# Casting the two weight matrices to bf16 inside their loads, on the GpSimd DMA queue, in a fused recurrence and feed-forward kernel

## The chip, the cores and the metric

The kernel runs on one core of a Trainium2 chip. The metric is the device time of one execution in microseconds (us). The kernel before took 201.83 us, the median of three runs (200.89 to 202.03).

Engine names in the profile: PE is TensorE, PEld its weight loads, DVE VectorE, ACT ScalarE, POOL GpSimd, SP SyncE. "L189" is line 189 of that kernel's source; the line numbers differ from kernel to kernel. All times inside a profile count from the start of the profiled span. For a program on one core, a run more than 1.5% above the fastest run of the same kernel is called slow.

## The reference

```python
# q, k, v, alpha: (4 batches, 8 heads, 768 steps, 48), float32
state = zeros((B, H, 48, 48))
for t in range(768):
    state = alpha[:, :, t, :, None] * state + einsum('bhd,bhe->bhde', k[:, :, t], v[:, :, t])
    y[:, :, t] = einsum('bhd,bhde->bhe', q[:, :, t], state)
x = y.transpose(0, 2, 1, 3).reshape(3072, 384)
h = x @ w_in                 # w_in: 384 x 2048, float32
r = maximum(h, 0)
out = (r * r) @ w_out        # w_out: 2048 x 384; out: 3072 x 384, float32
```

## The kernel before

The recurrence is computed in 24 chunks of 128 steps (6 for each batch). Chunk s gives 128 rows of x, which are kept transposed in `xT_big`. Each chunk needs four loads of 192 KB (alpha, q, k and v, called `at`, `qt`, `kt`, `vt`), in rows of 48 floats, which are 192 bytes. The first matmul (x by w_in) starts with a group of four chunks, so it needs chunks 0 to 3 and the first quarter of w_in.

A list scheduler in Python, `Plan`, holds every operation with an estimated duration and its dependencies, and decides the order on each engine. The DMA loads are issued in a fixed order:

```python
    def add_loads(s):                       # four loads of chunk s, on the SP queue
        ...
        for nm, src in srcs:                # at, qt, kt, vt
            def ld(nm=nm, src=src):
                d[nm] = loads.tile([P, H, D], FP32, name=nm)
                nc.sync.dma_start(out=d[nm], in_=src[b, c])
    ...
    DMA_ORDER = [0, 1, 2, 3, "i", "i", "i", 4, "i", "o", "o", 5, "o", "o"]
    for d in DMA_ORDER + [s for s in range(NT) if s not in DMA_ORDER]:
        if d == "i":
            load_w_in(len(w_in_ready))      # a quarter of w_in, 768 KB
        elif d == "o":
            load_w_out(len(w_out_ready))    # a quarter of w_out, 768 KB
        else:
            add_loads(d)
            add_chunk(d)
```

The weights come through float32 staging tiles and are cast to bf16 by VectorE or GpSimd, whichever the scheduler finds free:

```python
    def cast(dst, box, j, d, n):
        def e_cast():
            eng = nc.vector if op.eng == "DVE" else nc.gpsimd
            pin(eng.tensor_copy(dst, box["t"][:, j, :]))
        op = add({"DVE": 0.06 + n / 1840.0, "POOL": 0.05 + n / 660.0}, 0, e_cast, d, prio=1.0)
        return op

    def load_w_in(i):
        ...
        def ld():
            box["t"] = wload.tile([P, KT * d_ff // NWP], FP32, name="wst").rearrange(...)
            nc.sync.dma_start(out=box["t"], in_=w_in_r[:, :, sl])
        d = add("DMA", WLD, ld, lat=2.0)
        cs = []
        for j in range(KT):
            cs.append(cast(w_in_b[:, j, sl], box, j, d, 512))
        w_in_ready.append(cs)
    # load_w_out: the same with w_out and four casts of 128 x 384
```

## Time and profile before

| stage of the profiled span (199.3 us) | what happens | what limits it |
|---|---|---|
| 0 to 20 us | loads of chunks 0 to 3, and their recurrence | the chunk loads: 4.2 us for each chunk |
| 20 to 26.5 us | chain of chunk 3, first casts | chunk 3's chain, with casts inside it |
| 26.5 to 44 us | first group of the first matmul | TensorE, with some waits for VectorE |
| 44 us to the end | both matmuls, remaining chunks | TensorE |

The first view is the timeline of GpSimd in the kernel before. Its columns are start, duration, engine, source line, operation, written tile <- read tile with shapes, the count, and in brackets how long the engine sat idle just before and what ended that.

```profile
7.02 0.61 POOL L284 CAST vb<-vt 128x384 bf16<-128x384 f32 x1 [3.64 <-DMA vt<-in_v_dram]
11.23 0.79 POOL L284 CAST vb<-vt 128x384 bf16<-128x384 f32 x1 [3.60 <-DMA vt<-in_v_dram]
15.45 0.61 POOL L284 CAST vb<-vt 128x384 bf16<-128x384 f32 x1 [3.43 <-DMA vt<-in_v_dram]
19.87 0.51 POOL L284 CAST vb<-vt 128x384 bf16<-128x384 f32 x1 [3.81 <-DMA vt<-in_v_dram]
```

`vt` is the last load of each chunk, so these four casts show when chunks 0 to 3 were complete: every 4.2 us, 1.05 us for one load. GpSimd waits for data each time; the loads are the limit here.

The next view is the timeline of VectorE in the kernel before, in the two places where casts of weights stand in the way.

```profile
22.65 0.43 DVE L221 CAST w_in_b<-wst 128x512 bf16<-128x512 f32 x1 [0.88 <-DMA wst<-in_moe_w_in_dram]
22.99 1.28 DVE L353 TENSOR_TENSOR sm<-sc,utri_b 128x512 bf16<-128x512 f32 x2
25.03 1.18 DVE L221 CAST w_in_b<-wst 128x512 bf16<-128x512 f32 x2 [0.76 <-DMA wst<-in_moe_w_in_dram]
26.13 0.34 DVE L408 COPY xT_big<-bank 128x384 bf16<-128x384 bf16 x1
...
41.06 2.27 DVE L221 CAST w_out_b<-wst 128x384 bf16<-128x384 f32 x5
43.25 0.35 DVE L408 COPY xT_big<-bank 128x384 bf16<-128x384 bf16 x1
```

VectorE waits 0.88 us for a weight transfer in order to cast it, while chunk 3's `sm` work stands behind the cast. Two more casts hold `xT_big` of chunk 3 until 26.13, and five casts of w_out hold another `xT_big` until 43.25. What TensorE pays for it is in its timeline in the kernel before:

```profile
26.53 0.81 PE L189 MATMUL bank<-xT_big,w_in_b 128*128 128x512 bf16 x3 [0.58 <-DVE xT_big L408]
...
28.87 0.32 PE L189 MATMUL bank<-L_s,utri_b 128*128 128x384 bf16 x1 [0.24 <-ACT L_s L278]
...
41.46 0.32 PE L189 MATMUL bank<-w_out_b,gT 128*128 128x384 bf16 x1 [0.56 <-DVE w_out_b L221]
43.66 0.34 PE L189 MATMUL bank<-L_s,utri_b 128*128 128x384 bf16 x1 [1.87 <-DVE xT_big L408]
```

The first line is the start of the first matmul, at 26.53 (its view is cut at 27 us, so the count stops at 3). The second is the first work of chunk 4. From there to the end of the span are 172.8 us. TensorE is close to full in the long stage after that, as the table of stretches shows (stretch, length, busy time of PE, PEld, DVE, ACT and POOL with their counts, granted clock, DMA share, GB/s):

```profile
60.00:176.00 116.00, 115.39 (x1349) 88.96 (x1348) 85.13 (x161) 89.87 (x272) 75.05 (x122) 1.00 0.71 137
```

Two lines of the page of the kernel before complete the picture: the span, and the clock granted to TensorE in 40 slices of 5 us, in tenths. The 7 is the slice after the wait of 1.87 us.

```profile
span 199.3 us, 5199 instructions
...
PEclk9999999997999999999999999999999999999999
```

### The profile page before, as it was taken

How to read it: one execution, taken by the hardware profiler on the slowest of the kernel's cores; microseconds unless marked ns; L12 is line 12 of the kernel's file. 1: busy time of each engine (PE TensorE's matmuls, PEld its weight loads, DVE VectorE, ACT ScalarE, POOL GpSimd, SP SyncE). 2: the span in 40 equal slices, each digit the busy share in tenths (PEclk: the TensorE clock that was granted, in tenths of full speed). 3: DMA queues.
4: the chain of work that ended last, by engine and by line, in shares of the span. 5: the costliest groups of instructions: out<-in, count | busy, mean ns of one | idle time of the engine just before them, and what ended most of it. 6: DMA issues, size and time to landing. Idle time of an engine off the chain costs nothing.

```text
span 199.3 us, 5199 instructions
## 1 busy us (share of the span) xinstructions
PE 186.2 (93%) x1926; PEld 131.4 (66%) x1926; DVE 131.0 (66%) x253; ACT 129.1 (65%) x376; POOL 105.8 (53%) x175
## 2 busy tenths in 40 slices
PE   7887779959999999999999999999999999999993
PEld 2454434437667778778777777777777777777761
DVE  0598659987839969878786576677666766723300
ACT  3466148737158669977869778877877776656510
POOL 5111366844509518678557747756766565455300
PEclk9999999997999999999999999999999999999999
DMA  6999999999859999999998999971001101100122
GB/s 128 189 187 168 349 246 318 251 272 235 157 133 219 170 194 202 202 200 199 189 211 157 226 204 202 200 163 43 22 17 44 39 3 41 44 20 20 44 79 79
DMA packets 107034, 30.23 MB, mean 152 GB/s; under 512 B 100352, under 2 KB 105472, under 8 KB 107008
## 3 DMA queue, kind: packets, MB, share of 16 engines
q1 hardware_dynamic: 107008, 29.89, 73.2%
q8 instruction: 15, 0.25, 0.6%
q14 instruction: 11, 0.09, 0.2%
HBM read 25.17 MB, written 4.72 MB: 150 GB/s over the span
## 4 chain that ended last, share of the span: by engine, by line
PE 76%; SPq 9%; DVE 6%; DMA 5%; ACT 2%; issue 1%; ACTq 0%
PE bank L189 65%; SPq L264 8%; PE bank L192 6%; DMA at<-in_alpha_dram 5%; PE sc L189 3%; DVE w_out_b L221 2%; DVE gT L453 1%; PE st L189 1%; SPq L232 1%; ACT r L446 1%; DVE qkT L337 1%; DVE sm L353 1%; DVE w_in_b L221 1%; ACT A L301 0%; DVE kI_s L323 0%
## 5 line engine op out<-in xcount | busy, mean ns | idle before, releaser
L453 POOL TENSOR_TENSOR gT<-r 128x256 bf16<-128x256 bf16 (+2 forms) x128 | 83.9, 665 | 57.9 <-ACT r L446 55.8
L446 ACT ACTIVATE r<-bank 128x256 bf16<-128x256 f32 (+2 forms) x192 | 68.9, 387 | 28.2 <-PE bank L189 25.6
L189 PE MATMUL bank<-xT_big,w_in_b 128*128 128x256 bf16 (+2 forms) x576 | 81.7, 275 | 1.1 <-DVE xT_big L408 0.6
L189 PE MATMUL bank<-w_out_b,gT 128*128 128x384 bf16 x384 | 75.2, 328 | 0.6 <-DVE w_out_b L221 0.6
L189 PEld LDWEIGHTS <-w_in_b 128*128 128x128 bf16 x576 | 49.2, 99 | 14.9 <-issue 2.4
L189 PEld LDWEIGHTS <-gT 128*128 128x128 bf16 x384 | 36.6, 98 | 17.2 <-issue 0.3
L453 DVE TENSOR_TENSOR gT<-r 128x256 bf16<-128x256 bf16 (+2 forms) x64 | 29.1, 464 | 17.6 <-ACT r L446 15.5
L353 DVE TENSOR_TENSOR sm<-sc,utri_b 128x512 bf16<-128x512 f32 x48 | 31.0, 684 | 4.4 <-PE sc L189 3.9
L320 DVE TENSOR_TENSOR qA_s<-qt,A 128x384 bf16<-128x384 f32 x24 | 13.6, 568 | 16.6 <-ACT A L301 16.6
L284 POOL CAST vb<-vt 128x384 bf16<-128x384 f32 x24 | 13.7, 573 | 18.8 <-DMA vt<-in_v_dram 18.7
L337 DVE COPY qkT<-bank 128x1024 bf16<-128x1024 bf16 x24 | 16.4, 684 | 4.7 <-PE bank L192 4.3
L484 ACT COPY ob<-bank 128x384 f32<-128x384 f32 x19 | 9.1, 481 | 13.9 <-PE bank L189 12.9
L323 DVE TENSOR_TENSOR kI_s<-kt,Ainv 128x384 bf16<-128x384 f32 x24 | 16.8, 699 | 1.9 <-ACT Ainv L305 0.4
L189 PEld LDWEIGHTS <-qkT 64*128 64x128 bf16 (+1 forms) x272 | 11.0, 95 | 9.3 <-DVE qkT L337 3.7
L301 ACT ACTIVATE A<-bank 128x384 bf16<-128x384 f32 x24 | 11.8, 493 | 7.2 <-PE bank L189 7.2
L278 ACT ACTIVATE L_s<-at 128x384 bf16<-128x384 f32 x24 | 12.5, 522 | 5.0 <-DMA at<-in_alpha_dram 5.0
L397 ACT CAST xn<-bank 128x384 bf16<-128x384 f32 x24 | 11.5, 479 | 4.8 <-PE bank L189 4.7
L379 ACT CAST sb<-st 128x384 bf16<-128x384 f32 x20 | 9.6, 478 | 7.1 <-DVE st L374 7.0
L189 PE MATMUL bank<-warm 128*128 128x512 bf16 x38 | 11.9, 453 | 1.3 <-DVE ae_s L182 1.3
L408 DVE COPY xT_big<-bank 128x384 bf16<-128x384 bf16 x24 | 8.5, 352 | 5.7 <-PE bank L192 5.6
L305 ACT ACTIVATE Ainv<-bank 128x384 bf16<-128x384 f32 x24 | 11.9, 494 | 0.0
L189 PE MATMUL sc<-qkT 64*128 64x128 bf16 x192 | 9.5, 219 | 1.9 <-DVE qkT L337 1.8
(40 smaller groups left out, 150.1 us busy)
## 6 DMA issues: line engine op xcount, KB each, us to landing
at<-in_alpha_dram SPq DMA_DIRECT2D x24, 192.0 KB, 4.6
qt<-in_q_dram SPq DMA_DIRECT2D x24, 192.0 KB, 4.5
kt<-in_k_dram SPq DMA_DIRECT2D x24, 192.0 KB, 4.6
vt<-in_v_dram SPq DMA_DIRECT2D x24, 192.0 KB, 4.3
out_dram<-ob SPq DMA_DIRECT2D x24, 192.0 KB, 2.5
wst<-in_moe_w_in_dram SPq DMA_DIRECT2D x4, 768.0 KB, 6.5
wst<-in_moe_w_out_dram SPq DMA_DIRECT2D x4, 768.0 KB, 7.9
```

The costliest lines, as they stand in the source:

```text
L189: pin(nc.tensor.matmul(*a, **kw))
L192: pin(nc.tensor.transpose(*a))
L264: nc.sync.dma_start(out=d[nm], in_=src[b, c])
L278: pin(nc.scalar.activation(L[:, :, 0:D], d["at"], AF.Ln))
L284: pin(nc.gpsimd.tensor_copy(d["vb"], d["vt"]))
L305: pin(nc.scalar.activation(d["Ai"], d["pm"][:, 0:HD].rearrange("p (h d) -> p h d", h=H), AF.Exp, scale=-1.0))
L320: pin(nc.vector.tensor_mul(qA[:, :, 0:D], d["qt"], d["A"]))
L323: pin(nc.vector.tensor_mul(kI[:, :, 0:D], d["kt"], d["Ai"]))
L337: pin(nc.vector.tensor_copy(d["qkT"], d["pT"]))
L353: pin(nc.vector.tensor_mul(d["sm"][:, hh], d["sc"][:, hh], utri_b.to_broadcast([P, NP, P])))
L446: pin(nc.scalar.activation(box["r"][:, 0:n], box["ph"][:, 0:n], AF.Relu))
L453: pin(eng.tensor_mul(gT[g][:, f, 0:n], box["r"][:, 0:n], box["r"][:, 0:n]))
```

## The change

The idea is to drop work from VectorE and GpSimd. A DMA issued from GpSimd can convert its data, so w_in and w_out are loaded straight into the bf16 tiles. The 28 casts and the four staging tiles go away; 18 of the casts ran on VectorE and 10 on GpSimd. The Trainium skill ("DMA: Bandwidth & Descriptors", SWDGE vs HWDGE vs iDMA) lists the cast in a transfer as possible from GpSimd only, so the eight weight loads have to leave the SP queue.

```diff
-    wload = ctx.enter_context(tc.tile_pool(name="wload", bufs=4))
...
-    def cast(dst, box, j, d, n): ...
+    W_EARLY = 1.5
+    W_ISSUE = 1.0
+
+    def load_w(dst, src, ready):
+        def ld():
+            nc.gpsimd.dma_start(out=dst, in_=src)
+        d = add("DMA", WLD, ld, lat=2.2)
+        d.late = -W_EARLY
+        d.pool = W_ISSUE
+        ready.append([d])
 
     def load_w_in(i):
         w = d_ff // NWP
         sl = slice(i * w, (i + 1) * w)
-        box = {}
-        (staging tile, nc.sync.dma_start, three casts)
+        load_w(w_in_b[:, :, sl], w_in_r[:, :, sl], w_in_ready)
 
     def load_w_out(i):
         w = FT // NWP
-        (staging tile, nc.sync.dma_start, four casts)
+        sl = slice(i * w, (i + 1) * w)
+        load_w(w_out_b[:, sl, :], w_out_r[:, sl, :], w_out_ready)
```

(The lines in parentheses stand for code that is cut here. A few lines in the scheduler reserve 1 us of GpSimd for each issue.)

The plan still believes in one DMA queue in the order of `DMA_ORDER`, but the load instruction is not pinned to its place. In the compiled program GpSimd's order is: the v cast of chunk 0, w_in 0 and 1, the v cast of chunk 1, w_in 2 and 3, w_out 0 and 1, the v cast of chunk 2, w_out 2 and 3, then the rest. No load waits for anything except its place in this order.

## The prediction

> **What bounds it now.** Three stages (timeline, windows).
> - 0 to 20 us: the loads of chunks 0 to 3. The GpSimd timeline shows the four vb casts waiting for v at 7.0, 11.2, 15.45 and 19.9: 4.2 us per chunk, about 1.05 us per 192 KB load, at 188 GB/s. All run in 192 B pieces; the DMA row reads 9, so I take the transfer engines to be full.
> - 20 to 44 us: chunk 3's chain, then the first group of the first matmul, starting at 26.5 (wait on xT_big). Here the casts cost time. VectorE waits 0.88 us for a w_in transfer and casts it while chunk 3's sm work is ready, so sm starts at 23.0 instead of 21.8; two more casts hold xT_big to 26.1. I estimate 2 us lost before 26.5. From 32 to 40 VectorE is 8.00 of 8 us busy, and TensorE waits 0.56 and 1.87 us near 41 to 43.7. TensorE idle from 26.5 to 44: about 3.3 us.
> - 44 to 196: TensorE is full (115.4 of 116 us in 60 to 176) and is the chain. Nothing saved elsewhere counts there.
>
> **What changes.** 28 casts go: 18 on VectorE (about 10 us), 10 on GpSimd (about 7 us). At most about 5 us lies on the chain. The eight 768 KB weight loads leave the SP queue for the GpSimd queue; the source bytes stay. In the compiled order two w_in loads follow the first vb cast, w_in 2,3 and w_out 0,1 the second, w_out 2,3 the third, all without waits. So they issue from 7.6 us on, ahead of most of chunks 1 to 3; before, the first was issued at 17.0, behind all sixteen.
>
> The Trainium skill ("DMA: Bandwidth & Descriptors", Issuing engines are not separate DMA queues) says that all queues interleave on the same 16 engines. So the second queue brings no bandwidth; it takes away the order. One weight piece costs 2.2 us of all engines (w_in pieces landed at 22.65, 25.0, 27.2), so eight cost 17.8 us. Chunk 3 landed at 19.9; if the two queues share evenly in time it lands near 30; if 2 KB pieces alternate with 192 B pieces, near 37; if the small loads win, near 20. The matmul start follows about 4.5 us later: 34, 41 or 24.5. After that about 3.3 us of gaps are won back.
>
> Sum: even sharing 201.8 + 7.5 - 3.3 = 206; alternating pieces 213; small loads winning 197 to 198; a casting transfer that is itself slower, more.
>
> **Predicted: 207 us, 197 to 217 in 8 of 10. Faster by over 2%: 0.13; within 2%: 0.30; slower by over 2%: 0.57.**
>
> **What would show it.** vb casts waiting for v well after 11.2, 15.45 and 19.9 (chunk 3 at 28 to 37); first w_in matmul at 32 to 42, ending its wait on xT_big, not on weights; the DMA row above 200 GB/s from 9 us on. From there to the end about 167 us instead of 170: no 1.87 us gap, VectorE not full.
>
> **What would make it wrong.** The small loads may be limited by their descriptors' generation rather than by the engines; then weights fill free slots, the matmul starts near 24.5 to 26, and the result is 2 to 3% faster. Or the casting transfer is much slower than 2.2 us, and the matmul or the second matmul waits for w_in or w_out: slower than 213. Or TensorE, left idle, restarts at a lower clock (0.7 in the slice after the 1.87 us gap).

## More of the kernel before

Where a chunk's chain leaves TensorE idle in the plan, the kernel issues filler matmuls on a tile of zeros, called `warm`; they keep TensorE busy and compute nothing:

```python
            if pe_end is not None and DUMMY:
                n = max(0, int((op.start - pe_end - 0.5) / 0.22))
                ...
                for _ in range(n):
                    mm(wp, lhsT=warm[:, 0:P], rhs=warm, start=True, stop=True)
```

Two pools matter later: `loads` has 6 buffers for each of the four chunk tiles, and `opool` has 4 buffers of `ob`, the output tile of one block of 128 rows. The stores of `ob` are issued on the same SP queue as the chunk loads.

## The result, and the profile after

The changed kernel took 208.68 us, the median of four runs (208.39 to 208.82), and the kernel before 201.38 us over its four runs (200.89 to 202.03). The ratio is 1.035, with a 95% interval of 1.032 to 1.038: slower. Ratios here are formed from the fast runs alone, so they are not quite the ratios of the medians quoted.

GpSimd's timeline after the change, which answers to the four lines of before. The lines "DMA_DIRECT2D" are the issues of the weight loads.

```profile
7.11 0.50 POOL L270 CAST vb<-vt 128x384 bf16<-128x384 f32 x1 [3.73 <-DMA vt<-in_v_dram]
7.55 1.71 POOL L224 DMA_DIRECT2D w_in_b<-in_moe_w_in_dram  x2
11.15 0.50 POOL L270 CAST vb<-vt 128x384 bf16<-128x384 f32 x1 [1.89 <-DMA vt<-in_v_dram]
11.60 1.55 POOL L224 DMA_DIRECT2D w_in_b<-in_moe_w_in_dram  x2
13.15 1.52 POOL L224 DMA_DIRECT2D w_out_b<-in_moe_w_out_dram  x2
28.36 0.51 POOL L270 CAST vb<-vt 128x384 bf16<-128x384 f32 x1 [13.69 <-DMA vt<-in_v_dram]
28.81 1.48 POOL L224 DMA_DIRECT2D w_out_b<-in_moe_w_out_dram  x2
32.11 0.51 POOL L270 CAST vb<-vt 128x384 bf16<-128x384 f32 x1 [1.82 <-DMA vt<-in_v_dram]
```

Chunk 1 is complete as before, at 11.15. Six weight loads are then under way, and chunk 2 comes at 28.36 instead of 15.45, chunk 3 at 32.11 instead of 19.87. VectorE, which before was held up by casts, now waits for chunk 2 (its timeline after):

```profile
21.01 0.56 DVE L306 TENSOR_TENSOR qA_s<-qt,A 128x384 bf16<-128x384 f32 x1 [7.03 <-DMA qt<-in_q_dram]
26.47 0.56 DVE L309 TENSOR_TENSOR kI_s<-kt,Ainv 128x384 bf16<-128x384 f32 x1 [4.91 <-DMA kt<-in_k_dram]
...
37.69 0.36 DVE L394 COPY xT_big<-bank 128x384 bf16<-128x384 bf16 x1 [1.28 <-PE bank L193]
```

One load of 192 KB now lands 5.46 us after the one in front of it (q at 21.01, k at 26.47), where that took 1.05 us before. TensorE's timeline after shows the same waits and the start of the first matmul:

```profile
15.11 0.48 PE L190 MATMUL bank<-L_s,utri_b 128*128 128x384 bf16 x1 [2.60 <-ACT L_s L264]
...
21.62 0.61 PE L193 MATMUL bank<-ident_bf,qA_s 128*128 128x128 bf16 x4 [3.58 <-DVE qA_s L306]
...
27.09 0.61 PE L193 MATMUL bank<-ident_bf,kI_s 128*128 128x128 bf16 x4 [4.86 <-DVE kI_s L309]
...
38.10 2.10 PE L190 MATMUL bank<-xT_big,w_in_b 128*128 128x512 bf16 x9
```

The first matmul starts at 38.10, and it waits for no weight. The chain of work that ended last goes through the same place: two of its pieces in order of time (start, duration, what) follow; the first is chunk 2's v, 15.68 us from issue to landing:

```profile
12.63 15.68 DMA vt<-in_v_dram
28.31 0.05 issue
```

The span and the clock row of the page after the change:

```profile
span 207.0 us, 5206 instructions
...
PEclk9997556999999999999999999999999999999998
```

Three stretches of the table of stretches after the change, with the columns as before:

```profile
15.00:20.00 5.00, 2.93 (x21) 1.52 (x20) 0.00 (x0) 2.00 (x7) 0.00 (x0) 0.70 1.23 198
...
25.00:30.00 5.00, 2.00 (x20) 1.50 (x21) 2.02 (x5) 0.53 (x1) 1.64 (x3) 0.50 1.10 193
...
60.00:176.00 116.00, 115.30 (x1335) 87.57 (x1334) 82.36 (x157) 88.93 (x267) 67.62 (x111) 1.00 0.65 127
```

The granted clock is at one half from 21.4 to 35.0 us and in one earlier window (14.6 to 18.0), which fits the waits of 2.6 to 4.9 us above. The long stage is unchanged: 115.30 us of 116 busy, against 115.39.

The balance of the two profiled spans is therefore short. The first matmul starts 11.6 us later (38.10 against 26.53). From there to the end the new kernel takes 168.9 us against 172.8, so 3.9 us are won back: the wait of 1.87 us and its dip of the clock are gone, and VectorE is no longer full from 32 to 40 us. The sum is 7.7 us, the difference of the spans.

The trace also has a record for every DMA packet. A packet of a chunk load is one row of 192 bytes and took 18.2 ns on average. A packet of a staged w_in load was 2048 bytes and took 100.0 ns. In the converting load, the same 512 floats arrive as a record of 1024 written bytes and took 98.2 ns, and a w_out row (768 bytes written) 80.6 ns. These means are near each other because some staged packets took much longer than most; the medians are 84 ns staged and 96 ns converting. In four slices of 2 us, from 17.6 to 25.6 us, I counted 309, 320, 383 and 381 weight packets against 323, 333, 381 and 389 chunk packets. In that stretch the two queues were served packet for packet. Earlier they were not: in the slices from 11, 13 and 15 us, 234, 281 and 262 weight packets passed beside 563, 584 and 707 chunk packets, and the trace does not tell whether every engine had both kinds waiting there.

### The profile page after: what moved, and what is told of

The parts are those of the page before. It is cut to its first block, busy times and chain, and to the rows that moved or that the text cites. A ratio compares the mean times of both kernels' runs of the same rounds, so it can differ in the third digit from the quotient of the medians.

```text
span 207.0 us, 5206 instructions
## 1 busy us (share of the span) xinstructions
PE 186.5 (90%) x1924; PEld 132.0 (64%) x1924; DVE 121.6 (59%) x239; ACT 130.3 (63%) x380; POOL 98.5 (48%) x165
## 2 busy tenths in 40 slices
DMA packets 107034, 27.08 MB, mean 131 GB/s; under 512 B 100352, under 2 KB 107008, under 8 KB 107008
## 4 chain that ended last, share of the span: by engine, by line
PE 76%; DMA 8%; SPq 5%; ACT 5%; DVE 3%; issue 1%; POOL 0%; ACTq 0%; DVEq 0%
PE bank L190 65%; DMA vt<-in_v_dram 8%; PE bank L193 6%; SPq L250 5%; PE sc L190 3%; ACT r L432 2%; PE st L190 1%; DVE kI_s L309 1%; DVE qA_s L306 1%; ACT L_s L264 1%; ACT ob L470 1%; DVE st L360 1%; ACT sb L365 0%; ACT xn L383 0%; DVE qkT L323 0%
## 5 line engine op out<-in xcount | busy, mean ns | idle before, releaser
L439 POOL TENSOR_TENSOR gT<-r 128x256 bf16<-128x256 bf16 (+2 forms) x120 | 78.5, 664 | 67.4 <-ACT r L432 62.8
L190 PE MATMUL bank<-xT_big,w_in_b 128*128 128x256 bf16 (+2 forms) x576 | 80.3, 272 | 0.5 <-ACT r L432 0.4
L190 PEld LDWEIGHTS <-w_in_b 128*128 128x128 bf16 x576 | 48.3, 97 | 14.0 <-issue 1.3
L306 DVE TENSOR_TENSOR qA_s<-qt,A 128x384 bf16<-128x384 f32 x24 | 14.4, 599 | 25.5 <-ACT A L287 18.4
L270 POOL CAST vb<-vt 128x384 bf16<-128x384 f32 x24 | 12.4, 515 | 29.3 <-DMA vt<-in_v_dram 29.3
L470 ACT COPY ob<-bank 128x384 f32<-128x384 f32 x23 | 11.1, 484 | 13.1 <-PE bank L190 12.2
L383 ACT CAST xn<-bank 128x384 bf16<-128x384 f32 x24 | 11.6, 482 | 6.4 <-PE bank L190 6.4
L193 PE MATMUL bank<-ident_bf,kI_s 128*128 128x128 bf16 x96 | 9.8, 227 | 5.9 <-DVE kI_s L309 5.9
L193 PE MATMUL bank<-ident_bf,qA_s 128*128 128x128 bf16 x96 | 9.7, 227 | 3.8 <-DVE qA_s L306 3.8
```

The lines of the kernel that those rows point to most:

```text
L190: pin(nc.tensor.matmul(*a, **kw))
L193: pin(nc.tensor.transpose(*a))
L270: pin(nc.gpsimd.tensor_copy(d["vb"], d["vt"]))
L306: pin(nc.vector.tensor_mul(qA[:, :, 0:D], d["qt"], d["A"]))
L439: pin(eng.tensor_mul(gT[g][:, f, 0:n], box["r"][:, 0:n], box["r"][:, 0:n]))
L470: pin(nc.scalar.copy(box["ob"], box["po"]))
```

## The experiments

The main theory, "order": on a second queue the weight loads overtake chunks 2 to 4, and because packets of the two queues are taken in equal numbers, each small packet of a chunk waits for a large one of the weights. The first rival, "conversion": the converting transfer is slow in itself. The second rival, "generation": the small packets come slowly by themselves, whatever else is moving. The clock is a possible third contributor.

Several experiments read float32 weights in place: w_in and w_out are loaded unchanged, and the matmul reads the upper 16 bits of each float as bf16. This drops the lower 16 bits; every run below still gave a result that passed the comparison with the reference. The kernel before ran beside the experiments on the same chip: its median was 200.89 us beside e1 to e4, 200.67 beside e5 to e8, and 201.30 beside e9 to e11. The diffs of e1 to e9 are against the changed kernel, those of e10 and e11 against the kernel before; `d.pos` fixes the place of a load in the emitted order.

| run | what it is | median us | ratio to before (95%) | first matmul at, us |
|---|---|---|---|---|
| after | the change | 208.68 | 1.035 (1.032 to 1.038) | 38.10 |
| e1_casts_gone | no casts, order as before | 199.46 | 0.994 (0.988 to 0.999) | 26.02 |
| e2_plain_pool | GpSimd queue, no conversion | 210.87 | 1.049 (1.043 to 1.054) | 38.80 |
| e3_sp_early | one queue, weights early | 211.76 | 1.056 (1.049 to 1.062) | 37.31 |
| e4_late | the change, loads behind chunk 3 | 200.80 | 0.998 (0.993 to 1.004) | 28.09 |
| e5_after_warm | the change, TensorE kept busy | 207.52 | 1.034 (1.027 to 1.041) | 36.92 |
| e6_small_rows | the change, half-width w_in rows | 212.05 | 1.056 (1.048 to 1.064) | 42.44 |
| e7_ordered | loads in order, fillers | 201.65 | 1.005 (0.998 to 1.013) | 26.82 |
| e8_hybrid | w_in in place on SP, w_out converting | 200.59 | 0.997 (0.990 to 1.004) | 25.95 |
| e9_ordered_ob8 | e7 with 8 output tiles | 198.27 | 0.986 (0.982 to 0.991) | 27.45 |
| e10_inplace | before, w_in in place, fillers | 197.77 | 0.984 (0.979 to 0.988) | 25.94 |
| e11_inplace_nofill | the same without fillers | 197.65 | 0.985 (0.979 to 0.990) | 25.02 |

(The row of after was measured earlier, against 201.38 us of before. Medians are over all runs; e2 and e8 have one slow run each, and their fast runs alone have medians of 210.77 and 200.31 us. The starts of the first matmul are each from one profiled run.)

### e1: only the casts taken away

```diff
-    w_in_b = consts.tile([P, KT, d_ff], BF16)
-    w_out_b = consts.tile([P, FT, d_model], BF16)
+    w_in_f = consts.tile([P, KT, d_ff], FP32)
+    w_out_f = consts.tile([P, FT, d_model], FP32)
+    def halves(t):
+        return t.bitcast(BF16).rearrange("p k (f two) -> p k f two", two=2)[:, :, :, 1]
+    w_in_b = halves(w_in_f[:, :, :])
+    w_out_b = halves(w_out_f[:, :, :])
...
-            nc.gpsimd.dma_start(out=dst, in_=src)
+            nc.sync.dma_start(out=dst, in_=src)      # dst is the float32 tile
```

> The casts alone are taken away: the weights stay fp32 in SBUF, loaded by the same queue in the same order as before the change, and TensorE reads the upper two bytes of each element in place (a truncation instead of a rounding, so the result is less exact). My theory (the casts cost about 5 us on the chain, the order of the loads costs about 12): first w_in matmul at 24.5 to 25.5 us instead of 26.5, no 1.87 us gap near 42, total 196 to 198 us. Rival (the casts were off the chain and the gain inside the changed kernel has another source, such as the new order of instructions): 200 to 202 us. Check: w_in and w_out matmuls must keep their 0.216 us and 0.16 us pace, else the reading in place costs something itself.

It took 199.46 us, 0.6% under the kernel before (the interval, 0.988 to 0.999, just leaves out 1), and I expected 196 to 198; the first matmul came at 26.02, and I expected 24.5 to 25.5. Chunks came as before (v casts up to 20.23). Two things took the rest. TensorE waited 1.11 us for chunk 3's k and had one window of 3.41 us at half clock. And reading w_out in place is not free. These are the two matmul groups of this run (count, then busy us, mean ns of one, then idle before):

```profile
L195 PE MATMUL bank<-xT_big,w_in_f 128*128 128x256 bf16 (+2 forms) x576 | 80.5, 272 | 0.7 <-ACT r L435 0.6
L195 PE MATMUL bank<-w_out_f,gT 128*128 128x384 bf16 x384 | 77.4, 330 | 0.0
```

In the changed kernel, which reads packed bf16, the same groups are:

```profile
L190 PE MATMUL bank<-xT_big,w_in_b 128*128 128x256 bf16 (+2 forms) x576 | 80.3, 272 | 0.5 <-ACT r L432 0.4
L190 PE MATMUL bank<-w_out_b,gT 128*128 128x384 bf16 x384 | 74.8, 326 | 0.0
```

w_in is the stationary operand (`lhsT`) and its matmuls are unchanged. w_out is the moving operand, and its group is 2.6 us longer. From the first matmul (26.02) to the end of the span (197.3) this run takes 171.3 us against 172.8 before; without the 2.6 us it would be 168.7, an estimate that agrees with the 168.9 us of the change. This fits the reading that what the change won after its first matmul is what the casts had cost.

### e2: the second queue without the conversion

The loads stand at the same places of GpSimd's order as in the change, but they carry plain float32, read in place as in e1.

```diff
-            nc.gpsimd.dma_start(out=dst, in_=src)
+            pin(nc.gpsimd.dma_start(out=dst, in_=src))   # dst float32
+        d.pos = W_POS[...]   # W_POS = [7.6, 7.7, 11.9, 12.0, 12.1, 12.2, 16.1, 16.2]
```

> The changed kernel with the conversion taken out of the transfer: the same eight weight loads at the same places of the GpSimd queue, but plain fp32 into fp32 tiles read in place. My theory (the loads overtake chunks 2 to 4, the conversion is free): as the changed kernel, vb casts of chunks 2 and 3 at 28 and 32 us, first w_in matmul at 37 to 39, total 207 to 210 us. Rival (the converting transfer is what is slow): weight packets get clearly shorter, chunk 2 lands before 24 us, total under 204 us.

It took 210.87 us, a little over the 207 to 210 expected; the first matmul, at 38.80, came as expected. GpSimd's timeline gives chunks 2 and 3 within 0.4 us of the change:

```profile
28.74 0.51 POOL L277 CAST vb<-vt 128x384 bf16<-128x384 f32 x1 [14.07 <-DMA vt<-in_v_dram]
...
32.25 0.63 POOL L277 CAST vb<-vt 128x384 bf16<-128x384 f32 x1 [1.57 <-DMA vt<-in_v_dram]
```

The rival "conversion" falls: without any conversion the loss is the same, and the 2.2 us by which this run is longer than the change are about the price of reading w_out in place (2.6 us in e1; the two totals come from different calls). The records here are of 4096 and 4608 bytes, 189 and 219 ns each, and 171, 161 and 149 of them passed in three slices of 2 us beside 185, 175 and 164 chunk packets. So in this stretch it is the number of packets that is shared equally, not bytes and not time.

### e3: the early order on one queue

```diff
-    DMA_ORDER = [0, 1, 2, 3, "i", "i", "i", 4, "i", "o", "o", 5, "o", "o"]
+    DMA_ORDER = [0, 1, "i", "i", "i", "i", "o", "o", 2, 3, "o", "o", 4, 5]
```

Everything is on the SP queue, plain float32, read in place. The weights simply go first: in the trace no chunk packet was served between 12 and 22 us.

> No GpSimd queue and no conversion: plain loads on the SP queue, six weight loads put into its order before chunk 2 and two behind chunk 3 (read in place, as in e1). My theory (order alone): six pieces of 2.2 us stand before chunk 2, so the vb cast of chunk 2 comes at about 28.7 us, of chunk 3 at about 32.9, first w_in matmul at 37 to 38, total 207 to 210 us. Rival (the loss comes from the second queue, its software descriptors or GpSimd's time): with one queue it is gone, total 197 to 202 us.

It took 211.76 us, over the 207 to 210 expected (w_out is read in place here too, and TensorE waited 1.36 us more at 39.48, for alpha of chunk 4). The first matmul, at 37.31, came as expected, and chunks 2 and 3 came where one queue in this order puts them:

```profile
28.85 0.51 POOL L273 CAST vb<-vt 128x384 bf16<-128x384 f32 x1 [17.07 <-DMA vt<-in_v_dram]
32.67 0.51 POOL L273 CAST vb<-vt 128x384 bf16<-128x384 f32 x1 [3.31 <-DMA vt<-in_v_dram]
```

The change behaves like this kernel. That follows from its order: by the time chunk 2 is complete, six weight loads are complete too, whether they ran before the chunk's packets or between them. Six loads at 2.2 us are 13.2 us, and 15.45 + 13.2 gives 28.7 against 28.36 measured. "Generation" is answered by the change itself together with this run: chunk 3, with the engines to itself, takes 3.8 us here for four loads, and in the change a single load beside the weights takes 5.46 us. Small loads limited by their own generation would have kept their pace.

### e4: the change with its loads behind chunk 3

```diff
-            nc.gpsimd.dma_start(out=dst, in_=src)
+            pin(nc.gpsimd.dma_start(out=dst, in_=src))
+        d.pos = W_POS[...]   # all eight between 20.45 and 20.8, behind chunk 3's v cast
```

> The changed kernel with all eight casting loads held in GpSimd's order behind the vb cast of chunk 3. My theory (packets of the two queues alternate one for one): chunk 3's vb cast is back at 19.9 to 20.5 us, first w_in matmul at 25 to 26.5; but then chunk 4 on the SP queue shares packet for packet with the weights and lands only at 40 to 46 us, and TensorE, which has chunk 4's transposes in its fixed order, stalls some 5 to 8 us around 32 to 42; total 200 to 205 us. Rival A (only the loads before chunk 3 matter): total 195 to 198 us. Rival B (casting loads are slow wherever they stand): 207 us or more.

It took 200.80 us, the same as the kernel before within the interval. The loss is gone with the order alone: chunk 3 came at 20.71 (GpSimd's timeline). But now the first matmul waits for its weights, 2.91 us, and starts at 28.09 (TensorE's timeline), not at 25 to 26.5 as I expected; the clock is at one half from 28.3 to 31.7 us.

```profile
20.71 0.51 POOL L272 CAST vb<-vt 128x384 bf16<-128x384 f32 x1 [4.61 <-DMA vt<-in_v_dram]
...
28.09 3.80 PE L190 MATMUL bank<-xT_big,w_in_b 128*128 128x512 bf16 x9 [2.91 <-DMA w_in_b<-in_moe_w_in_dram]
```

My expectation that chunk 4 would come late, at 40 to 46 us, was wrong: most of its packets had passed before the first weight packet. The run also showed a later wait of 2.1 us for an output copy, which e7 explains.

### e5: the clock

```diff
+    def fill(n):
+        t = banks[4].tile([P, 512], FP32, name="bank4")
+        for _ in range(n):
+            mm(t, lhsT=warm[:, 0:P], rhs=warm, start=True, stop=True)
...     # for chunk 2 alone: fill(10), fill(15) and fill(20) in its three waits
```

> The changed kernel with 45 filler matmuls on data that is already there, put where TensorE waited for chunk 2's loads (10 before the prefix product, 15 before the transposes of q, 20 before those of k), so that it does not idle. They must not delay anything: the waits there were 2.6, 3.6 and 4.9 us. If the halved clock of 20 to 34 us lengthened chunk 3's chain, the granted clock stays at 1.0, the vb casts stay at 28.4 and 32.1 us, and the first w_in matmul moves from 38.1 to 36.6 to 37.0 us; total 1.0 to 1.5 us below the changed kernel's 208.7, so 207.0 to 207.7. Rival (the clock costs nothing there because the chain waits on other engines): start unchanged within 0.3 us.

It took 207.52 us. The clock stayed at full speed, as the table of stretches of this run shows (third column from the end):

```profile
20.00:25.00 5.00, 3.40 (x20) 1.51 (x18) 0.56 (x1) 0.00 (x0) 0.00 (x0) 1.00 1.26 185
25.00:30.00 5.00, 3.30 (x29) 1.73 (x28) 2.16 (x5) 0.57 (x2) 1.63 (x3) 1.00 0.98 174
```

The first matmul started at 36.92 instead of 38.10, inside what I expected. So the half clock is worth 1.2 us of the 11.6, and the late chunks the other 10.4. This rests on the profiled starts; the totals of this run and of the change come from different calls, and their ratios (1.034 and 1.035) do not tell 1.2 us apart. The Trainium skill ("TensorE: Matmul & The Clock Gate", Part 1) says that TensorE falls to half rate after at least one idle window of about 3.4 us. The change's trace agrees in part: before its last microseconds its time at 0.5 is one stretch of 3.41 us and one of four times that, and waits of 3.58 and 4.86 us stand at the second, but the first began in a wait of only 2.60 us.

### e6: half as wide weight packets

```diff
+            c = dst.shape[2] // parts        # parts = 2 for w_in, 1 for w_out
+            for i in range(parts):
+                pin(nc.gpsimd.dma_start(out=dst[:, :, i * c:(i + 1) * c], in_=src[:, :, i * c:(i + 1) * c]))
```

If packets are taken in equal numbers, a weight packet of half the length should cost a chunk packet half the wait, while the same bytes go over.

> The changed kernel with each w_in load cut in two of 256 columns, so that its packets carry half as much, at the same places. Theory (the engines take one packet of each queue in turn, so chunk loads get time by packet size): during the w_in loads a 192 KB chunk load takes 64 pairs of about 65 to 75 ns, 4.2 to 4.8 us, instead of the changed kernel's 5.5 to 6.5; qA_s of chunk 2 starts at 17 to 18.5 us instead of 21.0, kI_s at 22 to 24 instead of 26.5. Since the bytes are the same, chunk 2 is complete at 26 to 29 and the total stays within 1% of the changed kernel: 207 to 210.5 us. Rival (engine time is shared evenly, whatever the packet): qA_s and kI_s of chunk 2 within 0.7 us of 21.0 and 26.5.

For chunk 2 this came out in the main (two runs only). VectorE's timeline of this run has q at 17.24, in the expected range, and k at 21.56, a little before the expected 22 to 24, against 21.01 and 26.47 in the change:

```profile
17.24 0.56 DVE L310 TENSOR_TENSOR qA_s<-qt,A 128x384 bf16<-128x384 f32 x1 [3.28 <-DMA qt<-in_q_dram]
21.56 0.56 DVE L313 TENSOR_TENSOR kI_s<-kt,Ainv 128x384 bf16<-128x384 f32 x1 [3.77 <-DMA kt<-in_k_dram]
```

The records (59 ns) were again near one for one, from 13.6 to 21.6 us: 532, 507, 484 and 483 weight packets against 488, 509, 502 and 491. (Not in every stretch here either: from 31 to 33 us it was 504 against 66.) The total was a miss: 212.05 us, where I expected 207 to 210.5. Because chunk 2 was earlier, at 25.97, its v cast let the last two w_out loads go while chunk 3 was not yet in, and chunk 3 came only at 36.97. The harm moved from chunk 2 to chunk 3, and the first matmul to 42.44. By the estimate used for chunk 2 in e3, all eight loads ahead of chunk 3 give 19.87 + 8 x 2.2 = 37.5. What counts in the end is how many weight loads are ahead of the last chunk that the matmul needs.

### e7 and e9: the change with its order put right

```diff
+    # pinned: w_in 0 behind chunk 2's v cast, the others behind chunk 3's,
+    # w_out 2 and 3 behind the first square
+    W_POS = [16.1, 20.45, 20.5, 20.55, 20.6, 20.65, 28.0, 28.1]
...     # chunk 3 alone: fill(3); filler count from the gap less 0.3 instead of 0.5
```

> The change kept (casting loads from GpSimd, no staging, no casts) with the order put right: the first w_in piece behind the vb cast of chunk 2, the other three and two of w_out behind that of chunk 3, two of w_out one multiplication later; and a few filler matmuls for the clock. Theory: one piece (2.4 us of engine time) goes ahead of chunk 3, so vb of chunk 3 comes at 21.5 to 22.5 and the first w_in matmul at 26 to 27.5 at full clock, without e4's 2.9 us wait for w_in; from there 168.9 us of span as in the changed kernel, so 196 to 199 us. If instead it stays at e4's 200.8 or above, the alternation with chunks 4 and 5 costs more than I count.

It took 201.65 us; I expected 196 to 199. The start was as wanted: chunk 3 at 22.22, the first matmul at 26.82 without a wait. What failed came 42 us later. ScalarE's timeline of this run has this line:

```profile
71.37 0.48 ACT L479 COPY ob<-bank 128x384 f32<-128x384 f32 x1 [3.39 <-DMA out_dram<-ob]
```

TensorE's timeline of this run follows it half a microsecond later:

```profile
71.90 0.81 PE L190 MATMUL bank<-xT_big,w_in_b 128*128 128x256 bf16 x6 [3.10 <-ACT ob L479]
```

ScalarE waited for a store: all four `ob` tiles were full, because the first store was issued only at 67.0, in the SP queue behind chunk loads that had themselves come late. Then e9, the same with one number changed:

```diff
-    opool = ctx.enter_context(tc.tile_pool(name="opool", bufs=4))
+    opool = ctx.enter_context(tc.tile_pool(name="opool", bufs=8))
```

> e7 with eight instead of four output tiles. In e7 ScalarE waited 3.4 us at 68 to 71 us for an output tile, because the first stores stood behind chunk loads that the weights had delayed, and TensorE lost 3.1 us to it. Theory: that wait goes and nothing replaces it: total 3 us below e7's 201.65, so 198 to 199.3 us, about 1% under the kernel before. Rival (the stall only moves to the next late load): 200.5 or more.

It took 198.27 us, in the expected range and 1.4% under the kernel before. The wait is gone, and from the first matmul (27.45, TensorE's timeline of this run) to the end of its span (196.4) are 168.9 us, the same as in the change. This is the change with its benefit kept and its loss nearly removed: the first matmul is 0.9 us later than in the kernel before.

```profile
27.45 2.10 PE L190 MATMUL bank<-xT_big,w_in_b 128*128 128x512 bf16 x9
```

### e8: w_in in place on the SP queue, w_out converting on GpSimd

```diff
+    w_in_f = consts.tile([P, KT, d_ff], FP32)        # upper halves read in place
...
+            nc.sync.dma_start(out=w_in_f[:, :, sl], in_=w_in_r[:, :, sl])
+    W_POS = [28.0, 28.1, 31.0, 31.1]                 # w_out, behind the first squares
```

> w_in loaded as before on the SP queue in the old order, but kept in fp32 and read in place by the weight load (e1 showed the w_in matmuls at an unchanged 379 and 272 ns; the result is a truncation); w_out by casting loads on GpSimd, two behind the first multiplication of the second stage, two behind the next; fillers for the clock. No cast instruction is left and nothing overtakes chunks 0 to 3. Theory: first w_in matmul at 24.5 to 25.5, w_out matmuls at 326 ns, 168.9 us from there, total 194.5 to 197.5 us, the fastest of all. Rival (nothing beyond e1's 199.5 is to be had): 199 or more.

It took 200.59 us; I expected 194.5 to 197.5. The first matmul was early, at 25.95 (expected 24.5 to 25.5), but TensorE then waited 1.22 us for alpha of chunk 4 and 1.59 us for alpha of chunk 5. The second is the same mechanism, one stage later: in the slices from 36, 38 and 40 us, 362, 379 and 381 packets of w_out passed beside 337, 384 and 384 chunk packets. The first is not: the first packet of w_out came at 30.1, after that wait, and e10 and e11, which load nothing from GpSimd, wait 1.37 and 1.61 us at the same place.

### e10 and e11: the kernel before, with only w_in in place

w_in is stationary, and e1 showed that reading it in place costs nothing; w_out keeps its staging and its casts, and every load its place on the SP queue. e10 adds `fill(4)` in chunk 3; e11 does not.

```diff
-    w_in_b = consts.tile([P, KT, d_ff], BF16)
+    w_in_f = consts.tile([P, KT, d_ff], FP32)
+    w_in_b = w_in_f[:, :, :].bitcast(BF16).rearrange("p k (f two) -> p k f two", two=2)[:, :, :, 1]
...
-            box["t"] = wload.tile(...)
-            nc.sync.dma_start(out=box["t"], in_=w_in_r[:, :, sl])
+            nc.sync.dma_start(out=w_in_f[:, :, sl], in_=w_in_r[:, :, sl])
...
-        (three casts)
-        w_in_ready.append(cs)
+        w_in_ready.append([d])
```

> The kernel before with the w_in casts gone and nothing moved: w_in stays fp32, on the SP queue in the old order, and is read in place (truncated); w_out is staged and cast as before; four filler matmuls in chunk 3's wait for k keep the clock up. Theory: the w_in casts cost 1.5 to 2 us before the first w_in matmul, so it starts at 24.6 to 25.3 us at full clock, and the gap near 42 us is smaller; w_out matmuls stay at 326 ns; total 196 to 198 us, the fastest of all. Rival (chunk 3's chain waits on its loads, not on the casts): start at 26 us or later, total 199 to 201.

> e10 without the four fillers. As in e1 the granted clock should fall to a half for one 3.4 us window around 22 to 25 us; first w_in matmul 0.8 to 1.3 us later than in e10, total 0.8 to 1.3 us more. If the total is equal, the fillers are worth nothing.

They took 197.77 and 197.65 us, ratios 0.984 and 0.985. In e11 the first matmul started at 25.02 against 26.53, so the casts of w_in had held it up by 1.5 us. In e10 it started at 25.94, later than I expected; there the fillers stand in front of chunk 3's transposes of k (21.21, against 20.28 in e11). But the earlier start alone brought almost nothing, as TensorE's timeline of e11 shows:

```profile
25.02 2.10 PE L190 MATMUL bank<-xT_big,w_in_f 128*128 128x512 bf16 x9 [0.23 <-DVE xT_big L405]
28.73 0.32 PE L190 MATMUL bank<-L_s,utri_b 128*128 128x384 bf16 x1 [1.61 <-ACT L_s L275]
```

TensorE then waits 1.61 us for alpha of chunk 4 and begins that chunk at 28.73, against 28.87 before. Nearly all of the 3.3 us between the two spans (199.3 and 196.0) is won after that: the wait of 1.87 us near 42 us is one of 0.91, the wait of 0.56 before it is gone, and so is the half clock after it. The fillers were worth nothing, against my expectation of about one us: the profiled run of e11 kept the full clock without them. They may steady it, which is not settled: the two runs of e11 at a mean clock of 0.991 took 198.95 and 199.05 us, those at 1.0 took 196.91 to 197.72. The kernel before showed the same over 11 runs: 199.31 and 199.70 us at a mean clock of 1.0, up to 202.21 at 0.983. These two kernels and e9 are 1.4 to 1.6% under the kernel before, with intervals that exclude equality but not a gain of less than 2%, and far under the change; the intervals of the three overlap. e10 and e11 drop the lower bits of w_in, which e9 does not.

## Why the prediction was right or wrong

**The direction and its cause were right, and are shown.** The prediction said that the second queue takes away the order and brings no bandwidth. The Trainium skill's sentence behind it ("DMA: Bandwidth & Descriptors", Issuing engines are not separate DMA queues) agrees with this trace: v of chunk 2 came 12.9 us later although the bytes read are the same. e2 (no conversion, same loss), e3 (one queue in that order, same loss) and e4 (conversion, no loss with another order) separate order from conversion.

**The size: 207 predicted, 208.68 measured.** The sum was 201.8 + 7.5 - 3.3, and both terms were too small. The matmul start moved by 11.6 us, not 7.5, and 3.9 us were won back, not 3.3; in the spans 11.6 - 3.9 = 7.7, against 4.2 predicted. That the total is only 1.7 us off has another part: I rounded the sum of 206 up to 207, for the chance of alternating packets and of a slower transfer, and the median of the kernel before was 201.38 in the final set. So the closeness of the total is partly luck: two errors of opposite sign, in the sharing and in the count of loads (next paragraph), partly cancel.

**The term that was mis-sized is the sharing between the queues.** I took "if the two queues share evenly in time" for the central case. Where both queues were busy, the counts show equal numbers of packets instead, in the change, in e2 and in e6; with that sharing the prediction's own sum was 213. The Trainium skill (the same page, Queues, rings and completion order) says that each engine goes round-robin between queues at packet granularity, and that case was in the prediction as "if 2 KB pieces alternate with 192 B pieces, near 37". That case was too pessimistic in its own way: it put all eight weight loads ahead of chunk 3, but w_out 2 and 3 stand behind chunk 2's v cast, and that cast itself was late. Chunk 3 came at 32.11, after six loads (19.87 + 13.2 = 33.1 by the same estimate as for chunk 2). The compiled order had shown this, and I did not follow it into the time of chunk 2.

**The term "about 4.5 us later" held only at full clock.** From chunk 3's v to the first matmul the change took 5.99 us. With fillers (e5) it was 4.43, and in e3, where the clock was full, 4.64. The clock was named as a possible flaw and was not in the sum; e5 puts it at 1.2 us.

**The rivals in the prediction fell.** Small loads are not limited by the generation of their descriptors: they yielded to the weights, one for one from 17.6 us on, and a load that took 1.05 us took 5.46. The converting transfer is not what made the loss: e2 has the loss without conversion, the last weight packet came at 37.4 us in both, and no matmul waited for a weight in the change. A converting packet is somewhat slower, though: a row of 512 floats took 96 ns in the median, against 84 ns staged on the SP queue and 89 ns (half of a packet of 178 ns) in e2 on the same queue.

**The signs to look for.** Chunk 3 "at 28 to 37" and the first matmul "at 32 to 42" held (32.11, 38.10), as did the end of the 1.87 us gap. "The DMA row above 200 GB/s from 9 us on" was wrong: it read 198 in 15 to 20 us and 193 in 25 to 30. The total on the page fell from 30.23 to 27.08 MB, by just the half of the weights, so this view counts the bytes written, and a converting load shows half its reading. "About 167 us instead of 170" from the start of the first matmul to the end was 168.9 instead of 172.8, since I had not counted to the end of the span.

**What stays open.** The trace does not tell which of the 16 engines served a packet, so equal numbers in 2 us are shown, in the stretches named, and strict alternation of single packets is not; why the numbers were unequal from 11 to 17 us is open. In experiments with pinned loads the compiler also moved a few later stores against loads on the SP queue; e9 shows that the waits that came of it can be removed, but not how much of the last per cent it decides.

## What to carry to other kernels

A queue in order is a schedule: moving large transfers to a second queue gave them equal rights here with the small loads that the chain was waiting for, packet for packet where both queues were busy, and the queue with the smaller packets lost about four fifths of its rate (a load every 5.46 us instead of 1.05). When a load is moved to another issuing engine, read in the compiled order when it will be issued, and hold it behind something that marks the end of the urgent loads; then look for the next thing that sits in the same queue behind it, here the stores and their four tiles. Removing work from engines beside the critical one was worth what it had cost the chain, 3 to 4 us here, and no more; and an earlier start is worth little when the load needed next is not there yet (e11).

## What the Trainium skill lacked or had wrong

- "DMA: Bandwidth & Descriptors" (Queues, rings and completion order) gives a packet as typically 9 to 17 descriptors. In the trace a record of the SP queue was one row of 192 bytes, a record of a converting GpSimd load one row of 1024 or 768 written bytes, and a record of a plain GpSimd load 4096 or 4608 bytes, more than one row. From 17.6 to 25.6 us the queues were served in equal numbers of these records (309 against 323, 320 against 333, and so on); whether a record is a packet in the page's sense the trace does not say. The page does not draw the consequence for a queue of small rows: a 192 KB load went from 1.05 to 5.46 us.
- The same page (SWDGE vs HWDGE vs iDMA) says that a cast needs GpSimd, but not what the cast costs. Here a row of 512 floats took 96 ns in the median with the cast, against 89 ns without it on the same queue (e2) and 84 ns on the SP queue. In the arrival of chunks 2 and 3 this did not show (e2 against the change).
- No page that I read gives GpSimd's issue time for such a load: on average 0.74 to 0.86 us for each load of 768 KB when two were issued together, 0.93 us for one alone (e9).
- No page that I read gives a matmul's time when it reads bf16 as the upper halves of float32 in place; there is only a general rule on strides. As the stationary operand nothing (272 ns a matmul on average both ways), as the moving operand of 384 columns 330 against 326 ns, which was 2.6 us over 384 matmuls.
- "TensorE: Matmul & The Clock Gate" (Part 1) speaks, in its table of states, of at least one idle window of about 3.4 us before the rate is halved. In the kernel before a half-speed window of 3.41 us followed a wait of 1.87 us, and in e1 one came 1.7 us after a wait of 1.11 us. But in e7 the clock stayed at full speed through a wait of 3.10 us, and in e4 through one of 1.21 us. So the length of a single wait did not decide it here; what did is not shown.
